# Sparse attention and a Fourier mixing layer on one core: a new issue order for the first batch's attention, Fourier stage and weight conversion

## The chip, the cores and the metric

One Trainium2 chip, one core. The time is the device time of one execution of the program in microseconds (us), and the figure for a kernel is the median of its runs.

## What is computed

Four batches of 768 tokens. Attention first (8 heads of 64): each query sees the keys less than 16 tokens away, and one summary per block of 32 tokens (the maximum of the block's keys, the mean of its values). Then a Fourier mixing layer and a two-layer network over the 512 features:

```python
scores_all = concat([where(|i-j| < 16, q@k.T/8, -1e9), q@k_sum.T/8 + log(32)])
x  = softmax(scores_all) @ concat([v, v_sum])         # per head; heads side by side: (4, 768, 512)
u  = x + real(fft(fft(x, axis=1), axis=2))
un = (u - mean(u)) / sqrt(var(u) + 1e-6)
out = u + maximum(un @ w_ch1, 0) @ w_ch2              # w_ch1 512 x 2048, w_ch2 2048 x 512, float64 in memory
```

The two weight matrices arrive as float64, and the kernel makes float32 of them by integer operations.

## The kernel before

**Attention** (`gen_attention`, L757). A batch is done in four pairs of heads, g = 0 to 3, each in three steps. First come the scores: `sc` on TensorE, their exponential on ScalarE (`p`), and a multiplication by a 0/1 mask on VectorE. Then the block sums of the values (`sum_values`, L668, or `sum_scores`), after which the next pair is prepared: `prepare` (L619) transposes k and q on TensorE (`qk`, L631 in batch 0, L639 later), ScalarE copies them out, VectorE takes the block maxima `km` (L642). Last comes the value product `av` (L676, `wide_values` in batch 0), which VectorE divides by its row sums into `x`. Batch 0 uses a wide form of the scores with the mask `wide`, later batches a narrow form with the mask `near` and a tile `vs` whose last column is set at the start (L1128, L1129). In batch 0 each pair also issues two matmuls whose result nobody reads (`keep_busy`, L750).

**Block sums of v** (`block_sums`, L560). Four heads at a time: two loads `vb` and six additions on GpSimd (POOL) into `vbs`. The load of the sums (b, gg) is issued with the values of the pair before.

**Fourier stage** (`gen_fourier`, L889). VectorE folds x into even and odd parts, once for each parity `par` (`fold`, L899 to L912). TensorE multiplies by the sequence tables `fs` (`y`, L923, L927), ScalarE copies that out (`big`), TensorE multiplies by the feature table `fd` (`mx`, L944, L946), VectorE adds to x and takes the statistics (`bst`, `norm`). The result is normalized and transposed (`unt`, L982) into `u`.

**Network** (`gen_channel`, L989). Both products are done with Winograd's form of Strassen's scheme (seven products in place of eight). It has two halves, c = 0 and 1: first four blocks j of the hidden layer (`hx`, `hy`, `hz`, L1005), then their product with w2 added to x (`ox`, `oy`, `oz`, L1052). I call them "h c=0", "o c=0", "h c=1" and "o c=1".

**Weights** (`gen_weights`, L852). There are 16 blocks, `w1_0` to `w1_7` and `w2_0` to `w2_7`. A block is made of two pieces: a load `raw` of 512 KB, two integer operations on VectorE (L820, L821), two on ScalarE (L822, L823), two more on VectorE (L825, L827) and a multiplication; four additions follow for the block (`_left_sums` or `_right_sums`). `plan` (L791) gives the order, and for each block a stage of batch 0 ahead of which it isn't issued. Batch 0 uses a block as it is made; a store to DRAM keeps it for later batches, which load it again. Three w1 blocks and four w2 blocks fit; `raw` and `vb` share four buffers.

**What sets the order.** The code is a set of generators that `drive` (L1105) advances in turns: so many steps of each in a round, some with a priority some hundred instructions ahead. A compiler's list scheduler then puts each engine's instructions into one queue, by priority and by when it takes an instruction's inputs to be there. Nearly all transfers are issued by SyncE (SP) in one such queue; an instruction at its head that waits holds all behind it. At the end of the program the order of the stages is:

```python
drive((first(attn, 6), 1, 0))                                  # L1126: pairs 0 and 1 of batch 0
...
get_tables(0)
drive((attn, 1, 0), (first(weights, 18), 3, 0))                # pairs 2 and 3 beside the conversion
...
    drive((gen_fourier(0), 4, 600), (first(weights, 16), 3, 0), (first(attn, 5), 1, 0))   # batch 1's attention
    drive((gen_channel(0), 4, 0), (weights, 12, 0), (attn, 1, 0))
```

Of the kernel before, what the change touches and what calls it, by code (L numbers as in the profile page):

```python
# [478 lines left out]
def _main_program(ctx, tc, q, k, v, moe_w_ch1, moe_w_ch2, out):  # L479
# [54 lines left out]

    def abank(shape, name):
        return psum.tile(shape, FP, tag="attn", bufs=4, name=name)
# [11 lines left out]
    nat = {}  # L548

    def load(b, g):  # L550

        qn, kn = (apool.tile([P, 2, NST // 2, 2 * D], FP, tag="nat", bufs=4, name=f"{n}n_{b}_{g}") for n in "qk")
        for dst, src in ((kn, k), (qn, q)):
            nc.sync.dma_start(out=dst.rearrange("p e j n -> p (e j) n"),
                              in_=src[b, 2 * g:2 * g + 2].rearrange("e (j p s) d -> p (e j) (s d)", p=P, s=2))
        nat[b, g] = qn, kn
# [3 lines left out]
    def block_sums(b, gg):  # L560
# [3 lines left out]
        for i in range(2):  # L564
            nc.sync.dma_start(out=raw[i].rearrange("p f d -> p (f d)"),
                              in_=v[b, 4 * gg:4 * gg + 4].rearrange("h (n f) d -> (h n) (f d)", f=BLOCK)
                              [:, hf * D * i:hf * D * (i + 1)])
        gtt(raw[0], raw[0], raw[1], ADD)
        while hf > 2:
            hf //= 2  # L570
            gtt(raw[0][:, 0:hf], raw[0][:, 0:hf], raw[0][:, hf:2 * hf], ADD)
        vb = spool.tile([4 * nb, D], FP, tag="vbs", bufs=2, name=f"vbs_{b}_{gg}")
        gtt(vb, raw[0][:, 0], raw[0][:, 1], ADD)
# [14 lines left out]
    def load_wide_values(b, g):  # L588

        vw = wide_vw(g)  # L590
        for e in range(2):
            off = v[b, 2 * g + e].offset
            parts = [(W, WK, 0, NQ), (0, W, 1, NQ)] if (b, g, e) == (0, 0, 0) else [(0, WK, 0, NQ)]
            for r0, r1, i0, i1 in parts:
                nc.sync.dma_start(out=vw[r0:r1, e, i0:i1, 0:D],
                                  in_=bass.AP(v.tensor, off + (QB * i0 - W + r0) * D,
                                              [[D, r1 - r0], [QB * D, i1 - i0], [1, D]]))

    def load_narrow_values(b, g):
# [5 lines left out]
        for e in range(2):  # L605
            off = v[b, 2 * g + e].offset
            for h in range(2):
                r, i = 64 * (e ^ h), NB2 * h
                last = (b, g, e, h) == (B - 1, NP - 1, 1, 1)
                if last:  # L610

                    nc.sync.dma_start(out=vw[r + 64 - W:r + 64, i:nb - 1, 0:D],
# [3 lines left out]
                nc.sync.dma_start(out=vw[r:r + n, i:i + NB2, 0:D],  # L616
# [59 lines left out]
    def wide_values(b, g, p, x):  # L676
        vw = wide_vw(g)
        av = [abank([P, NST, D1], f"av_{b}_{g}_{e}") for e in range(2)]
        for n in range(NQ):
            for e in range(2):  # L680
                nc.tensor.matmul(av[e][QB * (n % 2):QB * (n % 2 + 1), n // 2, :], p[:, e, n, :], vw[:, e, n, :],
                                 start=True, stop=True)
        for e in range(2):
            rc = rec[:, b * NP + g, e]
            nc.vector.reciprocal(out=rc, in_=av[e][:, :, D])
# [64 lines left out]
    def keep_busy(b, g):  # L750


        ps = bank([P, 512], f"busy_{b}_{g}")
        for _ in range(2):
            nc.tensor.matmul(ps, ident, nat[b, g][:, 0:512], start=True, stop=True)

    def gen_attention(b):  # L757
        x = bpool.tile([P, NST, DM], FP, tag="x", bufs=2, name=f"x_{b}")
        x_of[b] = x
        for g in range(NP):  # L760
# [7 lines left out]
            if b == 0:  # L768
                keep_busy(b, g)
            if n1:  # L770
                prepare(*n1)
# [6 lines left out]
            if is_wide(b):  # L778
                wide_values(b, g, p, x)
            else:  # L780
                values(b, g, *p, x)
            if n2:
                load_values(*n2)
            yield
# [6 lines left out]
    plan = [(1, 0, None), (1, 1, None), (1, 2, None), (2, 0, None), (2, 1, ("y", 0)), (2, 2, ("y", 0)),  # L791
            (2, 3, ("mx", 0)), (1, 3, ("h", 0, 0)), (1, 4, ("h", 0, 1)), (1, 5, ("h", 0, 2)), (1, 6, ("h", 0, 3)),
# [4 lines left out]
    def load_raw(upto):  # L797
        for f, j, hh in pieces[len(raws):upto]:
# [8 lines left out]
            nc.sync.dma_start(out=raw.rearrange("p (a n) w -> p a (n w)", a=a), in_=src)  # L807
# [25 lines left out]
    def make(f, j):  # L833
# [13 lines left out]
        if len(stores) > 2 or len(pieces) == len(raws):  # L847
            nc.sync.dma_start(out=stores[0][0], in_=stores.pop(0)[1])
# [3 lines left out]
    def gen_weights():  # L852
        for f, j, stage in plan:
            while stage and stage not in issued:
                yield
            yield from make(f, j)
        for to, wv in stores:
            nc.sync.dma_start(out=to, in_=wv)

    def get_w1(b, j):  # L860
# [3 lines left out]
        nc.sync.dma_start(out=w, in_=dw1[j])  # L864
        wt[1, b, j] = w

    def get_w2(b, j):
# [3 lines left out]
        nc.sync.dma_start(out=w, in_=dw2[j])  # L871
# [5 lines left out]
    def get_tables(b):  # L877
        tag, bufs = ("w1", 3) if b else ("w2", NC)
        fs = []
        for par in range(2):  # L880
            t = bpool.tile([P, 2, HT, F2 + 1], FP, tag=tag, bufs=bufs, name=f"fs_{b}_{par}")
            nc.sync.dma_start(out=t, in_=dr["fs"].ap()[par])
            fs.append(t)
        fd = bpool.tile([P, 6, HD], FP, tag=tag, bufs=bufs, name=f"fd_{b}")
        nc.sync.dma_start(out=fd, in_=dr["fd"].ap())
        tables[b] = fs, fd
        return fs, fd

    def gen_fourier(b):  # L889
# [9 lines left out]
        for par in range(2):  # L899
            sd, zw, fg = fold[:, 0], fold[:, 1], fold[:, 2 - 2 * par]  # L900
            tt(sd, x[:, 0:HT, :], x[:, HT:NST, :], SUB if par else ADD)
            tt(zw[:, :, 0:HD], sd[:, :, 0:HD], sd[:, :, HD:DM], ADD)
            tt(zw[:, :, HD:DM], sd[:, :, 0:HD], sd[:, :, HD:DM], SUB)
            nc.vector.tensor_copy(out=zq[:, par], in_=zw[:, :, Q])
# [6 lines left out]
            nc.vector.tensor_copy(out=fg[:, :, DM - 1:DM], in_=zw[:, :, HD + Q:HD + Q + 1])  # L911
            fgs.append(fg)  # L912
            yield
        big = bpool.tile([P, NC, 2, S], FP, tag="h", name=f"big_{b}").rearrange("p j h s -> p (j h s)")
# [21 lines left out]
        for half in range(2):  # L936
# [28 lines left out]
            nc.vector.scalar_tensor_tensor(out=z, in0=stat[:, :, 0], scalar=-1.0, in1=y, op0=ALU.mult, op1=ALU.mult)  # L965
# [23 lines left out]
    def gen_channel(b):  # L989
        x, u = x_of[b], wt["u", b]  # L990
        for c in range(NJ // NC):
# [44 lines left out]
            for i in range(HT):  # L1036
# [35 lines left out]
                if NC * (c + 1) == NJ:  # L1072
                    for t in (i, HT + i):
                        nc.sync.dma_start(out=out[b, P * t:P * (t + 1), :], in_=x[:, t, :])
# [10 lines left out]
    load(0, 0)  # L1085
    nc.scalar.dma_start(out=count, in_=dr["count"].ap())
    nc.scalar.dma_start(out=wide, in_=dr["wide"].ap())
# [39 lines left out]
    nc.sync.dma_start(out=near, in_=dr["near"].ap().rearrange("p (h i) c -> p h i c", h=2))  # L1127
    nc.vector.memset(vs, 0.0)  # L1128
    nc.vector.tensor_scalar(out=vs[:, :, D], in0=half_of, scalar1=float(BLOCK), scalar2=None, op0=ALU.mult)  # L1129
    get_tables(0)  # L1130
    drive((attn, 1, 0), (first(weights, 18), 3, 0))
    for b in range(B):
        attn = gen_attention(b + 1) if b + 1 < B else iter(())
        if b == 0:
            drive((gen_fourier(0), 4, 600), (first(weights, 16), 3, 0), (first(attn, 5), 1, 0))
# [56 lines left out]
```

## Time and profile before

| | |
|---|---|
| median of 5 runs | 881.01 us |
| lowest, highest | 876.55, 888.2 us |
| the profiled execution | 888.29 us |
| its span, first to last instruction | 886.5 us |
| mean granted TensorE clock | 0.971 |
| TensorE busy | 829.2 us (94%) |
| VectorE busy | 499.5 us (56%) |
| ScalarE busy | 229.6 us (26%) |
| GpSimd busy | 47.9 us (5%) |
| first `y` matmul of batches 0, 1, 3 | 76.44, 305.91, 704.46 us |

Times in the profile count from the span's first instruction. A row of the timeline gives the start, the length, the engine, the line, the operation with the tile written and the tiles read, how many instructions are merged, and in brackets how long the engine had been idle and what ended that. In a table by stretches, (x12) is the number of instructions that began there, PEclk is the granted TensorE clock (1.00 is full), and the DMA share is that of the core's 16 DMA engines. One matmul on float32 counts as two or more instructions.

### The profile page before, as it was taken

The page shows a single profiled execution, that of the slowest core. Times are in us where ns is not written, and L with a number is a line of the kernel's source. Part 1 is how long each engine was busy: PE and PEld are TensorE (multiplying, and loading weights), DVE is VectorE, ACT ScalarE, POOL GpSimd, SP SyncE. Part 2 cuts the span into 40 slices and gives each one's busy share as a digit, 9 for nine tenths or more (in the row PEclk, how much of TensorE's full clock was granted, in tenths as well). Part 3 has the DMA queues.
Part 4 walks back from the last instruction along what each step waited for, and adds up shares of the span by engine and source line. Part 5 has one row for each costly group of instructions (what it writes and reads, how often), then busy time and mean ns, then how long its engine had stood idle before and what let it go on. Part 6 is the DMA issues. An engine that isn't in the chain of part 4 may idle for free. (4 is left out here: it accounts for less than half of the span.)

```text
span 886.5 us, 14658 instructions
## 1 busy us (share of the span) xinstructions
PE 829.2 (94%) x6122; PEld 612.7 (69%) x6122; DVE 499.5 (56%) x1107; ACT 229.6 (26%) x473; POOL 47.9 (5%) x48
## 2 busy tenths in 40 slices
PE   5976898899969998999999998999999989999997
PEld 3755665578538886678758886678758876687586
DVE  2479979796898347354329347353329355442352
ACT  2563354641530034312020034310120022101200
POOL 2400103002040000000000000000000000000000
PEclk8988979999998999999999999999999999999999
DMA  9997757893762284251531293220421261304001
GB/s 215 199 297 163 186 200 182 274 300 133 220 208 95 81 288 115 96 143 37 160 137 60 73 295 79 84 84 1 173 90 60 91 248 42 125 1 188 20 26 50
DMA packets 99915, 122.33 MB, mean 138 GB/s; under 512 B 50208, under 2 KB 83200, under 8 KB 99840
## 3 DMA queue, kind: packets, MB, share of 16 engines
q1 hardware_dynamic: 99152, 120.75, 46.1%
q8 instruction: 50, 0.82, 0.4%
q10 hardware_dynamic: 688, 0.56, 0.2%
q14 instruction: 25, 0.20, 0.1%
HBM read 100.32 MB, written 20.97 MB: 137 GB/s over the span
## 5 line engine op out<-in xcount | busy, mean ns | idle before, releaser
L1005 PE MATMUL hx<-u,w 128*128 128x384 f32 x512 | 186.5, 495 | 9.5 <-DVE h L542 4.2
L1005 PEld LDWEIGHTS hx<-u,w 128*128 128x128 f32 x512 | 95.7, 192 | 78.1 <-DVE h L542 7.8
L1005 PE MATMUL hz<-u,w 128*128 128x384 f32 x256 | 95.8, 493 | 3.3 <-ACT h L1022 2.3
L1052 PE MATMUL oz<-w,s 128*128 128x256 f32 x384 | 91.5, 379 | 0.0
L1052 PE MATMUL ox<-w,s 128*128 128x256 f32 x384 | 91.4, 381 | 0.0
L1052 PE MATMUL ox<-w,h 128*128 128x256 f32 x384 | 90.5, 384 | 0.0
L1052 PEld LDWEIGHTS ox<-w,h 128*128 128x128 f32 x384 | 74.0, 193 | 12.2 <-issue 0.6
L542 DVE TENSOR_TENSOR x<-ox,x 128x256 f32<-128x256 f32 x96 | 40.5, 423 | 71.8 <-PE ox L1052 71.6
L1052 PEld LDWEIGHTS ox<-w,s 128*128 128x128 f32 x384 | 72.2, 190 | 11.3 <-DVE x L542 1.4
L1052 PEld LDWEIGHTS oz<-w,s 128*128 128x128 f32 x384 | 72.9, 190 | 10.0
L1005 PEld LDWEIGHTS hz<-u,w 128*128 128x128 f32 x256 | 48.8, 192 | 37.9 <-ACT h L1022 3.0
L542 DVE TENSOR_TENSOR h<-hy,h 128x384 f32<-128x384 f32 x32 | 17.8, 555 | 60.6 <-PE hy L1005 60.6
L1005 PE MATMUL hy<-u,w 128*128 128x384 f32 x128 | 46.5, 486 | 0.0
L929 ACT COPY big<-y 128x192 f32<-128x192 f32 x32 | 10.7, 335 | 137.5 <-PE y L923 137.5
L542 DVE TENSOR_TENSOR h<-hx,h 128x384 f32<-128x384 f32 x32 | 17.8, 556 | 50.4 <-PE hx L1005 49.4
L1052 PE MATMUL oy<-w,h 128*128 128x256 f32 x192 | 45.6, 380 | 0.0
L923 PE MATMUL y<-fs,fold 128*128 128x193 f32 x192 | 36.7, 341 | 6.3 <-DVE fold L908 6.3
L1015 ACT COPY h<-hx 128x384 f32<-128x384 f32 x32 | 15.3, 479 | 98.3 <-PE hx L1005 94.0
L1052 PEld LDWEIGHTS oy<-w,h 128*128 128x128 f32 x192 | 36.5, 191 | 5.1
L923 PEld LDWEIGHTS y<-fs,fold 128*128 128x128 f32 x192 | 32.3, 195 | 9.4 <-DVE fold L908 6.5
L542 DVE TENSOR_TENSOR x<-oz,x 128x256 f32<-128x256 f32 x48 | 20.4, 424 | 32.8 <-PE oz L1052 32.7
L1031 ACT ACTIVATE h<-hx 128x384 f32<-128x384 f32 x32 | 15.7, 491 | 87.1 <-PE hx L1005 87.1
(115 smaller groups left out, 1106.7 us busy)
## 6 DMA issues: line engine op xcount, KB each, us to landing
w<-dw SPq DMA_DIRECT2D x48, 896.0 KB, 5.5
raw<-in_moe_w_ch_dram SPq DMA_DIRECT2D x32, 512.0 KB, 5.5
dw<-w SPq DMA_DIRECT2D x16, 896.0 KB, 7.0
vw<-in_v_dram SPq DMA_DIRECT2D x47, 192.0 KB, 4.9
kn<-in_k_dram SPq DMA_DIRECT2D x16, 384.0 KB, 5.7
qn<-in_q_dram SPq DMA_DIRECT2D x16, 384.0 KB, 6.4
vb<-in_v_dram SPq DMA_DIRECT2D x16, 384.0 KB, 5.2
out_dram<-x SPq DMA_DIRECT2D x24, 256.0 KB, 2.0
```

The source lines that it names most:

```text
L542: nc.vector.tensor_tensor(out=out, in0=in0, in1=in1, op=op)
L923: nc.tensor.matmul(y, fgs[par][:, st, P * g:P * (g + 1)], fs[par][:, g % 2, st, :], start=(st == 0), stop=(st == HT - 1))
L929: nc.scalar.copy(out=ty[:, g, par:S2:2], in_=y[:, 0:F2])
L1005: nc.tensor.matmul(ps, w[:, a, kk, :], u[:, r, kk, :], start=start and kk == 0, stop=stop and kk == 1, skip_group_check=True)
L1015: nc.scalar.copy(out=c11, in_=X)
L1031: nc.scalar.activation(out=c21, in_=X, func=AF.Relu)
L1052: nc.tensor.matmul(ps, left[a][:, n, :], wt[2, b, j][:, r, :], start=start and n == 0, stop=stop and n == NC - 1, skip_group_check=True)
```

## The change

- Batch 0's four `keep_busy` calls go. A new `keep_busy` issues two such matmuls after each of two folding steps of the first parity of batch 0's Fourier stage.
- For the last pair of batch 0, the value product is issued ahead of `prepare` of batch 1's first pair, and `tc.issue_after` puts that pair's TensorE instructions behind the last `av` matmul in TensorE's queue. It sets the order only; it adds no wait.
- Pairs 2 and 3 of batch 0 get a priority 600 ahead of the conversion. The second weight block is issued only behind the last folding instruction, and `w1_2`, `w2_0`, `w2_1`, `w2_2`, `w2_3` only behind the last instruction of the normalization (VectorE's queue; order only). `w1_3` moves ahead of `w2_1`.
- The block sums for batch 1 move from GpSimd to VectorE, as one addition and one `tensor_reduce`. Those of other batches stay.
- The setting of `vs` (L1128, L1129) is put behind pair 1's value product in VectorE's queue.
- Every transfer on SP up to the end of the first Fourier stage keeps the program's order (`tc.keep_in_program_order`). The first two raw loads move ahead to pair 0, the next two ahead of the tables; `near` goes behind the tables; `wide` moves from ScalarE's queue to SP's.

```diff
+    in_order = [True]
+    def fetch(out, in_):
+        ins = nc.sync.dma_start(out=out, in_=in_)
+        if in_order[0]:
+            tc.keep_in_program_order(ins)
...
         vb = spool.tile([4 * nb, D], FP, tag="vbs", bufs=2, name=f"vbs_{b}_{gg}")
-        gtt(vb, raw[0][:, 0], raw[0][:, 1], ADD)
+        if b == 1:
+            tt(raw[0], raw[0], raw[1], ADD)
+            nc.vector.tensor_reduce(out=vb, in_=raw[0].rearrange("p f d -> p d f"), op=ADD, axis=AX.X)
+        else:
+            gtt(raw[0], raw[0], raw[1], ADD)
...
+        marks["last av"] = ins.ins
...
-    def keep_busy(b, g):
-        ps = bank([P, 512], f"busy_{b}_{g}")
-        for _ in range(2):
-            nc.tensor.matmul(ps, ident, nat[b, g][:, 0:512], start=True, stop=True)
...
-            if b == 0:
-                keep_busy(b, g)
+            early = (b, g) == (0, NP - 1)
+            if early:
+                wide_values(b, g, p, x)
             if n1:
-                prepare(*n1)
+                with tc.issue_after(marks["last av"]) if early else ExitStack():
+                    prepare(*n1)
...
             if n2:
                 load_values(*n2)
+            if (b, g) == (0, 0):
+                load_raw(2)
...
-    plan = [(1, 0, None), (1, 1, None), (1, 2, None), (2, 0, None), (2, 1, ("y", 0)), (2, 2, ("y", 0)),
-            (2, 3, ("mx", 0)), (1, 3, ("h", 0, 0)), (1, 4, ("h", 0, 1)), ...
+    plan = [(1, 0, None), (1, 1, ("fold", 0)), (1, 2, ("mx", 0)), (2, 0, ("mx", 0)), (1, 3, ("h", 0, 0)), (2, 1, ("mx", 0)),
+            (2, 2, ("mx", 0)), (2, 3, ("mx", 0)), (1, 4, ("h", 0, 1)), ...
...
-            yield from make(f, j)
+            steps = make(f, j)
+            while True:
+                with tc.issue_after(marks[stage]) if stage in marks else ExitStack():
+                    done = next(steps, steps) is steps
...
+    def keep_busy(b, par, t):
+        if (b, par) == (0, 0):
+            ps = bank([P, DM], "busy")
+            for i in range(2):
+                nc.tensor.matmul(ps, ident, t[:, i, :], start=True, stop=True)
...
             tt(sd, x[:, 0:HT, :], x[:, HT:NST, :], SUB if par else ADD)
+            keep_busy(b, par, sd)
             tt(zw[:, :, 0:HD], sd[:, :, 0:HD], sd[:, :, HD:DM], ADD)
             tt(zw[:, :, HD:DM], sd[:, :, 0:HD], sd[:, :, HD:DM], SUB)
+            keep_busy(b, par, zw)
...
+        marks["fold", b] = ins.ins
+        issued.add(("fold", b))
...
     load(0, 0)
+    fetch(out=wide, in_=dr["wide"].ap())
     nc.scalar.dma_start(out=count, in_=dr["count"].ap())
-    nc.scalar.dma_start(out=wide, in_=dr["wide"].ap())
...
     drive((first(attn, 6), 1, 0))
-    nc.sync.dma_start(out=near, in_=dr["near"].ap().rearrange("p (h i) c -> p h i c", h=2))
-    nc.vector.memset(vs, 0.0)
-    nc.vector.tensor_scalar(out=vs[:, :, D], in0=half_of, scalar1=float(BLOCK), scalar2=None, op0=ALU.mult)
+    with tc.issue_after(marks["av", 0, 1]):
+        nc.vector.memset(vs, 0.0)
+        nc.vector.tensor_scalar(out=vs[:, :, D], in0=half_of, scalar1=float(BLOCK), scalar2=None, op0=ALU.mult)
+    load_raw(4)
     get_tables(0)
-    drive((attn, 1, 0), (first(weights, 18), 3, 0))
+    fetch(out=near, in_=dr["near"].ap().rearrange("p (h i) c -> p h i c", h=2))
+    drive((attn, 1, 600), (first(weights, 18), 3, 0))
...
-            drive((gen_fourier(0), 4, 600), (first(weights, 16), 3, 0), (first(attn, 5), 1, 0))
+            drive((gen_fourier(0), 4, 600), (first(weights, 66), 12, 0), (first(attn, 5), 1, 0))
+            in_order[0] = False
             drive((gen_channel(0), 4, 0), (weights, 12, 0), (attn, 1, 0))
```

All other `nc.sync.dma_start` calls of this program become `fetch` with the same arguments. `marks` also records the first reciprocal after each value product and the last instruction of the normalization.

## The prediction, made before the changed kernel was run

> **What bounds the kernel now.** First the page: engine totals, then the slices.
>
> ```profile
> PE 829.2 (94%) x6122; PEld 612.7 (69%) x6122; DVE 499.5 (56%) x1107; ACT 229.6 (26%) x473; POOL 47.9 (5%) x48
> ...
> DVE  2479979796898347354329347353329355442352
> PEclk8988979999998999999999999999999999999999
> ```
>
> A slice is 22.2 us. TensorE bounds the whole, but in slices 3 to 12 (about 45 to 265 us) VectorE is full, and the granted clock is lowest there. The first `y` matmuls of batches 1 and 2 are 198.6 us apart (305.91, 504.46); from batch 0's (76.44) to batch 1's it is 229.5 us. So the loss sits in the first 306 us. The table by stretches says where:
>
> ```profile
> 20.00:40.00 20.00, 20.00 (x298) 14.55 (x300) 7.49 (x16) 9.08 (x17) 7.65 (x7) 0.95 0.94 188
> 40.00:53.00 13.00, 13.00 (x194) 9.20 (x191) 7.06 (x12) 6.49 (x13) 3.31 (x5) 1.00 1.06 335
> 53.00:70.00 17.00, 10.57 (x171) 7.68 (x169) 15.72 (x36) 11.81 (x20) 0.14 (x1) 0.80 1.22 255
> 70.00:90.00 20.00, 13.72 (x68) 10.93 (x66) 19.47 (x35) 7.73 (x21) 3.04 (x2) 0.83 0.73 145
> 90.00:122.00 32.00, 28.11 (x304) 23.51 (x304) 26.30 (x78) 12.18 (x25) 2.88 (x4) 0.79 0.64 175
> 122.00:160.00 38.00, 34.30 (x294) 19.49 (x296) 33.44 (x63) 19.86 (x41) 8.68 (x5) 0.96 0.77 225
> 160.00:187.00 27.00, 23.66 (x293) 14.65 (x285) 24.82 (x55) 19.29 (x37) 0.00 (x0) 1.00 0.91 253
> 187.00:220.00 33.00, 33.00 (x158) 28.79 (x161) 25.47 (x56) 6.41 (x11) 5.13 (x5) 1.00 0.65 212
> 220.00:268.00 48.00, 40.81 (x221) 23.30 (x221) 42.30 (x79) 22.23 (x43) 10.79 (x8) 0.96 0.69 214
> ```
>
> The columns after the length are PE, PEld, DVE, ACT, POOL busy. Until 53 us TensorE has no gap and VectorE is idle over half the time (batch 0's attention). From 53 to 90 us TensorE is idle 12.7 of 37 us while VectorE is full: conversion competes with the end of attention and the fold. From 122 to 187 us both are nearly full; TensorE idles 7.0 us. In 187 to 220 us TensorE is full ("o c=0") and VectorE idles 7.5 us. The timeline shows what starts late:
>
> ```profile
> 12.21 1.99 DVE L1129 TENSOR_SCALAR vs<-half 128x2 f32<-128x2 f32 x1 [10.88 <-DMA half<-c_half]
> 15.11 1.35 PE L662 MATMUL sc<-qt,km 64*32 64x384 f32 x4 [3.96 <-DVE km L642]
> 31.68 1.98 PE L755 MATMUL busy<-qt,ident 128*128 128x512 f32 x4
> 48.15 1.24 PE L658 MATMUL sc<-qt,kt 64*96 64x64 f32 x24
> 57.65 0.85 PE L639 MATMUL qk<-ident,kn 128*128 128x128 f32 x6 [3.31 <-ACT cvt L822]
> 59.87 1.51 PE L639 MATMUL qk<-ident,qn 128*128 128x128 f32 x6 [1.37 <-DMA qn<-in_q_dram]
> 62.50 2.87 PE L681 MATMUL av<-vw,p 128*64 128x65 f32 x46 [0.57 <-ACT kt L641]
> 69.67 1.75 DVE L542 TENSOR_TENSOR fold<-x 128x1536 f32<-128x1536 f32 x1
> 76.44 2.94 PE L923 MATMUL y<-fs,fold 128*128 128x193 f32 x8 [6.28 <-DVE fold L908]
> 86.88 2.35 POOL L545 TENSOR_TENSOR vb<-vb,vb 96x1024 f32<-96x1024 f32 x1 [21.32 <-DMA vb<-in_v_dram]
> 86.91 2.61 DVE L821 TENSOR_SCALAR cvt<-raw 128x512 int32<-128x512 int32 x1
> ```
>
> A load that isn't needed (`half`) holds VectorE's queue, so the first `km` is 4 us late. The last `av` stands behind batch 1's `qk`, whose k and q are still in flight (`qn`, issued at 50.13, lands at 59.87; `kn`, issued 2.1 us ahead of it, fits 57.6, so I don't believe the ACT step named). The fold waits for that `av`, then `y` for the fold. And while POOL adds, a VectorE step of 0.42 us takes 2.61.
>
> **What the Trainium skill says.** "SBUF — State Buffer", section "Who interferes with whom": VectorE and GpSimd share a port pair under an exclusive lock, and `tensor_reduce` on trn2 never contends. The trace agrees on the lock (0.42 against 2.61 us); it has no `tensor_reduce` beside POOL work. "TensorE: Matmul & The Clock Gate", Part 1: after an idle window of about 3.4 us the clock is halved until a busy one. The trace agrees: after 6.28 us idle, 8 `y` matmuls take 2.94 us, against 1.58 in batch 3. "DMA: Bandwidth & Descriptors", section "Issuing engines are not separate DMA queues": transfers from ScalarE's and SP's queues share the same 16 engines, so moving `wide` should save issue time only. The before trace can't test that.
>
> **The change, part by part.**
>
> *Start and pair 0.* Without L1129 ahead, `km` is ready at 9.1 us instead of 15.1, and the first pair's scores end 4 us earlier. `keep_busy` of pair 0 is 3.06 us more. But the block sums now come last: POOL ends them at 17.25, so `vs` moves from 22.92 only to about 17.3. Gain 5.6. *Pairs 1 and 2*: a period is 10.33 us with TensorE gapless, ScalarE at 4.9 and VectorE at 4.3 us; taking out 1.98 us leaves TensorE the bound: 2 x 1.98 = 4.0. Scores of pair 3 start at 48.15 - 9.6 = 38.6.
>
> *Pair 3.* Its `vw` copy ends 6.3 us after its scores start; `av` 1.6 and the division 1.3 follow: x is complete 9.2 us after, against 69.4 - 48.15 = 21.3 now. Gain 12.1; sum 21.7. The cover to check is DMA. Up to pair 3's values SP must bring k, q 3.1 MB, v 2.4, block loads 2.4, `wide` and `sel` 0.5, and now the first raw pieces 1.0 ahead of them: 9.4 MB, landing at 40 us with the mean 235 GB/s, at 50 with the 188 of the slow stretch; needed at 45. I allow 2 us: x complete at 49.7, lead 19.7.
>
> *Fold and `y`.* The first parity's fold takes about 5 us without foreign work (6.8 less 2.3 that was mixed in): `y` starts at 55. The two new `keep_busy` calls (4 us) lie in TensorE's gap. The second parity follows at 62.5, `y` ends at about 68, against 88.9. Then `mx` to the end of normalization takes 17 us in batch 3 (715 to 731.6), undisturbed, against 27.4 here (88.5 to 116). I take 18.5 for `w1_1` and the block sums beside it: 86.5, and with 6 us of transposes the network starts at 93 instead of 121.7. Lead 28.7.
>
> *What is owed.* A block costs VectorE 2 x (0.42 + 0.42 + 0.69 + 0.68 + 0.68) + 4 x 0.42 = 7.5 us. Eight pieces, four blocks, are converted before 121.7 now. With the new plan it is `w1_0` (in attention's idle VectorE time), `w1_1`, and some 0.4 of `w1_2`: 2.4 blocks. The 1.6 missing ones cost 12 us where VectorE is full. Lead 16.7 when the eighth block is ready (now 163).
>
> *After that.* With `w1_3` ahead of `w2_1` to `w2_3`, the last block of "h c=0" no longer waits for all eight, and `w1_4` to `w1_6` slide under "o c=0", where VectorE idles 7.5 us. I take 5.5 (0 to 7.5). From "o c=0" on (220 to 268) nothing changes: the w2 buffers come free only then. Lead 22.2.
>
> *Edits at about nothing.* Batch 1's sums on VectorE: 1.2 us (1024 at the 1.75/1536 of the fold row) plus 1.25 (from 0.95 for the 768 of the `km` row), twice. The first pair lies in idle time; the second replaces 3.8 us that POOL's lock now adds at 86.9 to 92. Without that cover: 2.5. `near` is needed first at about 60. New waits: on SP the third raw load waits for a buffer and behind it stand tables, `near`, and batch 1's k, q and v; `y` and `qk` would wait. On VectorE the second sum may wait for its load with the fold behind it. Both between 0 and 10 us; I take 0 beyond the 2 allowed.
>
> Sum against the profiled execution: 888.3 - 22 = 866. It lies 7.3 us over the median; the parts are differences of one trace, so from 881 I get 859.
>
> **The rivals.**
> *More passes through.* If VectorE, full from 50 us, loses fewer gaps than the 13% it idles between 60 and 268 us now, the debt shrinks: at 5% idle it saves another 10 (8% of the 125 us from 93 to about 218): 849. For it: uncontended stages fill better. Against: `norm`'s short steps and buffer waits stay. The ceiling is TensorE, 55 + 198.6, far off.
> *The front is held by loads.* `kn` of batch 1 stands behind tables and raw pieces, and `y` behind its `qk`: x is in time, but `y` starts at about 65, and half the lead is lost: 870. For it: `qn` took 9.7 us here.
> *The clock.* Without `keep_busy` gaps halve the clock in pairs 1 to 3: each has 6.4 us of matmuls without queueing, doubled that is 3 x 6.4 = 19 us more: 859 + 19 = 878. Against: TensorE stays gapless by the sums above.
> *Slower: SP's fixed order serializes the pieces.* In the fixed stretch six pieces (`w1_1`, `w1_2`, `w2_0`) are loaded; if each load sits behind a waiting transfer of batch 1 until the conversion before it is done, each exposes its 5.5 us landing: 6 x 5.5 = 33, 892. Four exposed pieces cancel the gain, six make it slower. Against: four buffers let two to three pieces run ahead.
>
> **How the numbers follow.** The sum 45%, more through 25%, loads 15%, clock 7%, serialized 8%. About 1% (8.8 us) is what a measurement of this kernel can tell from no change. Faster: 45 + 25 + 12 of the loads' 15 = 82%; same: the clock's 7 and the loads' other 3, 10%; slower 8%. The range leaves out the serialized case, the clock and part of the edges: low 845 (more through, plus 4), high 873 (loads, plus 3).
>
> **What would show it.** Right: last `av` of batch 0 ahead of `qk` at about 45 us; fold at 50, `y` at 55 with no conversion between; first `hx` at about 93; first `ox` near 150; batch 1's `y` near 284. Wrong: a VectorE or SP wait on `vb` or `raw` over 5 us between 45 and 90, or a clock under 0.9 before 45.

## The result, and the profile after

The changed kernel takes 880.15 us (median of 42 runs, 876.5 to 885.53), the kernel before 882.0 us (median of 79 runs beside it, 871.61 to 888.69). The ratio is 1.000, with a 95% interval of 0.9988 to 1.0013 (the two medians alone give 0.998): no change, or 2 us at most, where I forecast 859. The changed kernel's profiled execution has a span of 878.8 us. Ratios everywhere, and the median of *early only*, leave out slow runs, those more than 1.5% above the fastest of their kernel.

The profiled execution of the kernel before that the prediction used (span 886.5) lies 6 us over its kernel's median. I ran that kernel again unchanged ("before again": 882.81 us, span 881.0) and compare with this second trace wherever it matters. Its first `y` of batch 1 comes at 300.6 us, where the first trace has 305.9 and the changed kernel 300.1: what looked like a gain of 5.8 us in the first batch is a difference between two executions of one kernel.

The page of the changed kernel: engine totals, then the slices of 22 us.

```profile
PE 823.1 (94%) x6114; PEld 608.2 (69%) x6114; DVE 505.4 (58%) x1111; ACT 229.5 (26%) x473; POOL 36.7 (4%) x38
...
DVE  3588996899999257353239247354329355442252
PEclk9979999799999999999999999999999999999999
```

TensorE's busy time and share hardly move. VectorE is still nearly full from slice 3 to slice 13, to about 290 us. The table by stretches, with the same columns as in the prediction:

```profile
40.00:53.00 13.00, 12.68 (x154) 9.35 (x156) 8.66 (x20) 7.54 (x13) 0.14 (x1) 0.87 0.58 129
53.00:70.00 17.00, 11.44 (x79) 7.66 (x80) 16.97 (x33) 2.33 (x7) 0.14 (x1) 0.80 1.07 281
70.00:90.00 20.00, 19.22 (x163) 15.48 (x165) 16.04 (x32) 7.92 (x22) 0.00 (x0) 1.00 0.90 173
90.00:122.00 32.00, 29.57 (x442) 20.33 (x436) 29.72 (x81) 22.67 (x44) 0.00 (x0) 0.95 0.77 213
122.00:160.00 38.00, 33.24 (x303) 19.58 (x302) 30.01 (x58) 20.87 (x41) 6.02 (x5) 0.96 0.68 188
160.00:187.00 27.00, 21.75 (x177) 15.12 (x177) 23.50 (x54) 12.94 (x24) 0.00 (x0) 0.81 0.99 276
220.00:268.00 48.00, 44.68 (x155) 28.55 (x153) 45.74 (x89) 22.39 (x43) 5.38 (x4) 1.00 0.76 254
```

From 70 to 122 us TensorE now idles 3.2 us where it idled 10.2, at a higher clock. From 160 to 187 it is worse: 21.75 us busy where it was 23.66, at clock 0.81 where it was 1.00. The timeline of the same execution:

```profile
18.20 0.52 PE L685 MATMUL vs<-vbs,sel 96*32 96x64 f32 x4 [4.75 <-POOL vbs L553]
...
53.26 1.90 DVE L580 TENSOR_REDUCE vbs<-vb 96x64 f32<-96x1024 f32 x1
...
57.95 1.75 DVE L550 TENSOR_TENSOR fold<-x 128x1536 f32<-128x1536 f32 x1
...
59.75 4.31 PE L914 MATMUL busy<-fold,ident 128*128 128x512 f32 x6 [5.56 <-DVE fold L550]
...
63.69 0.16 DVE L940 COPY fold<-fold 128x3 f32<-128x3 f32 x1
...
63.90 1.15 PE L954 MATMUL y<-fs,fold 128*128 128x193 f32 x6
...
130.74 2.53 POOL L553 TENSOR_TENSOR vb<-vb,vb 96x1024 f32<-96x1024 f32 x1 [76.33 <-DVE cvt L839]
...
130.98 2.85 DVE L550 TENSOR_TENSOR w<-cvt 128x512 f32<-128x512 f32 x1
...
137.92 2.93 PE L1038 MATMUL hx<-u,w 128*128 128x384 f32 x4 [3.08 <-ACT h L1048]
...
148.99 0.95 DVE L655 TENSOR_REDUCE km<-kt 128x24 f32<-128x768 f32 x1 [4.06 <-ACT kt L654]
...
171.24 0.90 PE L652 MATMUL qk<-ident,kn 128*128 128x128 f32 x3 [1.78 <-ACT kt L654]
...
171.94 2.77 PE L1038 MATMUL hx<-u,w 128*128 128x384 f32 x4
...
277.58 3.62 PE L1085 MATMUL ox<-w,s 128*128 128x256 f32 x8 [3.71 <-DVE x L550]
```

The fold starts at 57.95 (before 69.67) and `y` at 63.9 (before 76.44), so the front is earlier. Later come the losses: a VectorE step (L550, `w`) of 2.85 us beside GpSimd's sum, and TensorE waiting 3.08 us soon after it; VectorE standing 4.06 us behind `km`; TensorE waiting on ScalarE's `kt` and then running at half clock (four `hx` instructions in 2.77 us, where 1.56 us is usual; the four at 137.92 the same); and 3.71 us of waiting in "o c=1".

Milestones of the three traces, in us (first or last matmul of the stage, from the timeline):

| | before, shown | before again | after | lead on "again" |
|---|---|---|---|---|
| first `y` | 76.4 | 76.0 | 63.9 | 12.1 |
| last `y` ends | 88.9 | 88.3 | 80.0 | 8.3 |
| first `hx` | 121.7 | 121.0 | 106.2 | 14.8 |
| first `ox` (o c=0) | 175.5 | 174.8 | 158.4 | 16.4 |
| "o c=0" ends | 220.0 | 219.3 | 216.0 | 3.3 |
| "h c=1" ends | 268.2 | 262.4 | 255.6 | 6.8 |
| batch 1's first `y` | 305.9 | 300.6 | 300.1 | 0.5 |

The lead is there until the first `ox`. Inside "o c=0" 13.1 us of it go. About 2 of these are moved work: the value products of batch 1's last pair, which the kernel before runs just behind that stage, lie inside it in the changed kernel. "h c=1" gives 3.5 back, and "o c=1" takes 6.3.

A ledger shows what kind of loss this is. In each stretch of 4 us I take TensorE's loss as the stretch's length less the product of busy time and granted clock, and sum it up to 300 us:

| trace | loss to 120 us | loss 120 to 300 us | sum | span |
|---|---|---|---|---|
| before, shown | 39.6 | 19.1 | 58.7 | 886.5 |
| before again | 40.0 | 13.7 | 53.7 | 881.0 |
| after | 25.1 | 25.3 | 50.3 | 878.8 |

Against before again the front takes 14.9 us of loss out, and 11.6 us come back. The stretches in which they come back are 160 to 180 us (8.2 against 2.5), 120 to 140 (4.2 against 1.4) and 260 to 280 (6.9 against 2.7); the others sum to 1.2 us the other way. The first trace has 6.5 us in the last of these, so there the ledger alone proves nothing. The milestones do: from the end of "h c=1" to the first `y` the changed kernel takes 44.5 us, and both traces of the kernel before about 38.

### The profile page after: what moved, and what is told of

The parts are those of the page before. It is cut to its first block, busy times and chain, and to the rows that moved or that the text cites. A ratio compares the mean times of both kernels' runs of the same rounds, so it can differ in the third digit from the quotient of the medians.

```text
span 878.8 us, 14637 instructions
## 1 busy us (share of the span) xinstructions
PE 823.1 (94%) x6114; PEld 608.2 (69%) x6114; DVE 505.4 (58%) x1111; ACT 229.5 (26%) x473; POOL 36.7 (4%) x38
## 5 line engine op out<-in xcount | busy, mean ns | idle before, releaser
L1085 PE MATMUL ox<-w,s 128*128 128x256 f32 x384 | 93.5, 387 | 5.2 <-DVE x L550 5.2
L550 DVE TENSOR_TENSOR x<-ox,x 128x256 f32<-128x256 f32 x96 | 40.3, 421 | 69.3 <-PE ox L1085 69.1
L550 DVE TENSOR_TENSOR h<-hy,h 128x384 f32<-128x384 f32 x32 | 17.8, 556 | 61.0 <-PE hy L1038 60.9
L550 DVE TENSOR_TENSOR h<-hx,h 128x384 f32<-128x384 f32 x32 | 17.8, 556 | 48.2 <-PE hx L1038 48.2
L655 DVE TENSOR_REDUCE km<-kt 128x24 f32<-128x768 f32 x16 | 15.2, 951 | 45.7 <-ACT kt L654 32.8
L1064 ACT ACTIVATE h<-hx 128x384 f32<-128x384 f32 x32 | 15.7, 490 | 85.8 <-PE hx L1038 85.8
L550 DVE TENSOR_TENSOR x<-oz,x 128x256 f32<-128x256 f32 x48 | 20.3, 423 | 30.9 <-PE oz L1085 30.9
```

The lines of the kernel that those rows point to most:

```text
L550: nc.vector.tensor_tensor(out=out, in0=in0, in1=in1, op=op)
L655: nc.vector.tensor_reduce(out=km[:, 0:nb], in_=kt[:, W:W + S].rearrange("p (n f) -> p n f", f=BLOCK), op=ALU.max, axis=AX.X)
L1064: nc.scalar.activation(out=c21, in_=X, func=AF.Relu)
L1085: nc.tensor.matmul(ps, left[a][:, n, :], wt[2, b, j][:, r, :], start=start and n == 0, stop=stop and n == NC - 1, skip_group_check=True)
```

## The experiments

**First theory: the withheld conversion is a debt on VectorE.** At the first `hx` the kernel before has converted eight pieces, the changed one four, and the sixteenth piece is ready at 166.3 (165.6 in before again) and 166.2 us. (I count a piece as ready at the end of its last step before the multiplication.) A lead of 15 us would be paid with two blocks of 7.5 us. *light before* and *light after* leave the conversion out of both kernels:

```diff
-        nc.vector.tensor_scalar(out=ex, in0=high, scalar1=0x7FF00000, scalar2=None, op0=ALU.bitwise_and)
...
-        tt(dst, tmp[:, 1, :], tmp[:, 0, :], ALU.mult)
+        nc.vector.tensor_scalar(out=dst, in0=raws[i].bitcast(FP)[:, :, 1], scalar1=0.01, scalar2=None, op0=ALU.mult)
```

Of *before again* (the kernel before, unchanged):

> The kernel before, unchanged, for a second profile, because its profiled execution lay 7 us over its median and batch 1's first y matmul at 305.91 us there against 300.09 in the changed kernel. Theory (the change gains nothing because the conversion owed is paid back on VectorE): batch 1's y at about 300 to 302 us, and the sixteenth converted piece at about 165 us as in the first profile. Rival (the change gained 5.8 us in the first batch and lost it later): y at 305 to 306 again.

Of *light before*:

> The kernel before with the conversion left out: in place of its seven steps per piece, VectorE multiplies the high half of each number, read as a float32, by 0.01 (one step of about 0.4 us), so the weights are not the reference's; loads, sums and stores stay. It takes 32 x 2.5 = 79 us off VectorE. Theory: the first batch is bound by VectorE's conversion, so this is 15 to 35 us faster than before (about 850 to 866). Rival (the first batch is bound by TensorE and its order): under 8 us faster.

Of *light after*:

> The changed kernel with the conversion left out in the same way. Theory (the lead of 15.5 us at the first hx is lost only because two blocks more are still to be converted): with nothing owed the lead stays, and this is 10 to 16 us faster than the kernel before with the conversion left out. Rival (the lead is lost to TensorE's own work, which is merely done in another order): within 4 us of it.

Measured: light before 862.65 us, ratio to before 0.977 [0.9727, 0.9813]; light after 862.78, ratio 0.9767 [0.9717, 0.9817]. Conversion beside the rest costs about 20 us in one kernel and 17 in the other. My expectation for light after missed, but the run does not test the debt by its total: its front lost 33.0 us up to 120 where the changed kernel lost 25.1, so that it had no lead at its first `hx` (112.9 against 109.8).

*owed light* tests the debt itself. Only the four pieces that the changed kernel has not converted at its first `hx` (`w1_2`, `w2_0`) are made light:

```diff
+        if 4 <= i < 8:
...
+            nc.vector.tensor_scalar(out=dst, in0=raw.bitcast(FP)[:, :, 1], scalar1=0.01, scalar2=None, op0=ALU.mult)
...
+            return
```

> The changed kernel, with one multiplication in place of the seven steps for the four pieces of w1_2 and w2_0 (those weights are then not the reference's). These four pieces are the ones that the kernel before has done ahead of its first hx and the changed kernel has not. Theory (the lead at the first hx is eaten by these pieces on VectorE): first hx stays within 3 us of 106, the time from the first hx to batch 1's first y falls from 193.9 us to 178-182, total 863-869 us. Rival (the stretch is longer for other reasons: the order of batch 1's attention, the clock): at least 188 us for that stretch, total 875-880.

Measured: 879.54 us, ratio 0.998 [0.9963, 0.9997]; 192.1 us from the first `hx` to batch 1's first `y` (193.9 in the changed kernel). The theory fell: both figures are the rival's. A piece needs 0.42 + 0.42 + 0.69 + 0.68 + 0.68 = 2.89 us of VectorE, a light one 0.42, so four pieces free 9.9 us; yet the sixteenth piece comes at 164.2, only 2.0 us earlier. VectorE's waits from 104 to 168 us tell why:

```profile
DVE h L550 <- PE hx L1044: 7.4, 2, 3.9
DVE km L655 <- ACT kt L654: 4.1, 1, 4.1
```

In the changed kernel the same two rows are 1.9 and 4.1 us; all of VectorE's waits in this time sum to 15.7 us here and 9.0 there. VectorE's queue is fixed, and `h` additions and a `km` stand in it ahead of the next pieces; without the four pieces VectorE waits there for TensorE and ScalarE. Most of the freed time turns into waiting.

**The front alone.** *early only* is the kernel before with a single edit of the change, the last value product ahead of batch 1's keys.

```diff
+            early = (b, g) == (0, NP - 1)
+            if early:
+                wide_values(b, g, p, x)
...
```

> The kernel before with one part of the change: the last value product of batch 0 ahead of batch 1's keys. Theory: x is complete 3-6 us earlier and so is the first y, but VectorE has the same conversion left; the lead at the first hx is under 4 us and batch 1's first y moves by under 2 us: total 879-885 us. Rival (an earlier x is worth its full amount): 875-878.

Measured: 886.5 us, ratio 1.005 [1.0021, 1.0079], slower, which neither case of the expectation had. The first `y` is at 63.6, as early as with the whole change, but the first piece of weights is converted at 70.2 (before 56.5) and the sixteenth at 177.1 (before 166.3), and the first `ox` comes at 185.2 (before 175.5). Here an earlier fold pushed the conversion back, and the network waited for it.

*ungated* keeps the change but no longer withholds conversion:

```diff
-    plan = [(1, 0, None), (1, 1, ("fold", 0)), (1, 2, ("mx", 0)), (2, 0, ("mx", 0)), (1, 3, ("h", 0, 0)), (2, 1, ("mx", 0)),
-            (2, 2, ("mx", 0)), (2, 3, ("mx", 0)), ...
+    plan = [(1, 0, None), (1, 1, None), (1, 2, None), (2, 0, None), (1, 3, ("h", 0, 0)), (2, 1, ("y", 0)),
+            (2, 2, ("y", 0)), (2, 3, ("mx", 0)), ...
```

> The changed kernel with the stages of the plan as before (w1_1, w1_2, w2_0 without a stage, w2_1 and w2_2 behind y), so conversion is no longer withheld from the fold and the normalization; the order of blocks and all else stay. Theory (a piece costs VectorE 3.75 us wherever it is put): first hx moves later by about 3.7 us for each piece done ahead of it, 110-120 us, batch 1's first y and the total stay: 877-884 us. Rival 1 (withholding leaves VectorE idle 4 us in 70-90): 873-877. Rival 2 (the withheld conversion is what gives the front its worth): 886 or more.

Measured: 887.54 us (879.77 to 891.82), ratio 1.005 [1.0027, 1.0072]; its profiled execution (881.07) is among its lowest and can't show where the typical one loses. Rival 2 of the expectation holds: withholding conversion is worth some 7 us to this front by the medians, and 4 by the ratios.

**Which stall eats the lead in "o c=0"?** *w2 light* makes the six pieces of `w2_1` to `w2_3` light (`10 <= i < 16` in the edit of owed light).

> The changed kernel with one multiplication in place of the seven steps for the six pieces of w2_1, w2_2 and w2_3 (those weights are then not the reference's). Theory (o c=0 starts at 158 us with only part of its w2 blocks there, and TensorE meanwhile runs batch 1's last pair alone): the three blocks are there by 155, TensorE's loss to gaps and clock at 160-200 falls from 9.7 us to under 4, total 868-874. Rival (as with the owed pieces, less conversion only leaves VectorE waiting in its queue): loss at 160-200 of 8 or more, total 877-881.

Measured: 872.07 us, ratio 0.9887 [0.9863, 0.9911]. The stretch of "o c=0" in it:

```profile
160.00:187.00 27.00, 25.98 (x215) 21.21 (x215) 25.82 (x58) 10.10 (x19) 0.00 (x0) 1.00 0.94 271
```

TensorE is busy 25.98 us at full clock, where the changed kernel has 21.75 at 0.81. Six pieces free 14.8 us of VectorE and the total falls by 8; four pieces of the blocks before them freed 9.9 and gave about 1. So "o c=0" starts at 158 us with two of its four w2 blocks there, and TensorE then runs batch 1's last pair of heads, one short product after another, each waiting on ScalarE or VectorE. That the late blocks are what it waits for is argued from their times; the run also gives VectorE the 14.8 us for other work. (The last light piece is written at 159.4, not by 155 as expected.)

*w1_3 last* puts `w1_3` behind `w2_3` again:

```diff
-    plan = [..., (1, 3, ("h", 0, 0)), (2, 1, ("mx", 0)), (2, 2, ("mx", 0)), (2, 3, ("mx", 0)), ...
+    plan = [..., (2, 1, ("mx", 0)), (2, 2, ("mx", 0)), (2, 3, ("mx", 0)), (1, 3, ("h", 0, 0)), ...
```

> The changed kernel with w1_3 behind w2_3 again, as in the kernel before. My step 'After that' gave this move the larger part of 5.5 us. If so: 882-886. Theory (the eighth block comes at the same time whichever is last, and the loss is only shifted from h c=0 to o c=0): h c=0 ends 8-14 us later, o c=0 is 8-14 us shorter, total 876-882. Rival (with all w2 blocks there o c=0 runs without gaps and the lead survives): 868-874.

Measured: 880.28 us, ratio 0.9969 [0.9952, 0.9986]. The first `ox` moves from 158.4 to 173.5, so "h c=0" ends later than the expected 8 to 14 us, and "o c=0" is 8.6 us shorter (49.0 against 57.6). TensorE now waits once, 8.25 us at 146.55 in "h c=0". The total says that the order of these blocks only decides in which stage the eighth one is waited for.

*km after 12* moves one instruction: `km`, behind which VectorE stood 4.06 us, goes behind the twelfth piece.

```diff
-        nc.vector.tensor_reduce(...
+        with tc.issue_after(marks["piece", 11]) if (b, g) == (1, 3) and ("piece", 11) in marks else ExitStack(): nc.vector.tensor_reduce(
...
```

> The changed kernel with one instruction moved: in VectorE's queue the block maxima km of batch 1's last pair, which wait for kt until 149 us, go behind the twelfth piece's conversion instead of ahead of it (TensorE's order is the same instruction for instruction). Theory (VectorE's queue stands still behind km, and w2_1 to w2_3 with it): piece 12 done by 141-146 us instead of 153, piece 16 by 157-162 instead of 166, batch 1's first y 2-5 us earlier, total 875-879. Rival (the loss of 8 us at 160-180 lies in TensorE's own order, where batch 1's attention stands alone): batch 1's first y within 1.5 us of 300, total 879-882.

Measured: 880.31 us, ratio 0.9973 [0.9961, 0.9984]. The twelfth piece ends at 151.7 instead of 153.1, because the wait only changed its name: VectorE's next step of that piece waits 5.68 us for ScalarE (L834), which copies `kt` and `qt` first. The figures are the rival's, but the run removes one of two stalls in series, so it decides nothing between the theories.

*wprio* gives the conversion a priority of 300 in batch 0's network stage, and so puts it ahead of attention on all engines:

```diff
-            drive((gen_channel(0), 4, 0), (weights, 12, 0), (attn, 1, 0))
+            drive((gen_channel(0), 4, 0), (weights, 12, 300), (attn, 1, 0))
```

> The changed kernel with conversion 300 ahead in priority in the network stage of batch 0, so that the rest of batch 1's attention comes behind it on all engines (its last km behind the twenty-second piece). Theory (attention put ahead of conversion and alone on TensorE eats the lead): eighth block by 150-160 us, TensorE's loss to gaps and clock at 160-180 falls from 8 to under 4 us, total 868-876. Rival (the same losses come back where the attention then stands, in o c=1 and batch 1's Fourier stage): 877-885.

Measured: 890.42 us, ratio 1.0088 [1.0063, 1.0113], slower than either case of the expectation. The sixteenth piece is ready at 157.8, 8.4 us earlier, as the theory wanted, but TensorE's own order has not followed:

```profile
176.78 1.46 PE L727 MATMUL ss<-qt,km 64*32 64x384 f32 x2 [15.76 <-DVE km L655]
```

TensorE waits 15.76 us for the `km` that now stands behind eleven more pieces. With batch 3's sums on VectorE as well (below) this kernel takes 887.7, ratio 1.0048 [1.0032, 1.0064], slower than all three cases of its expectation:

> wprio_300 with batch 3's block sums on VectorE too. If both theories hold the gains add: 862-870 us. If priority of the conversion is worth nothing, the gain of the sums alone stays: 873-877. If the later attention takes the place where the sums gained, 875-881.

**The block sums, and GpSimd's lock.** The change moves only batch 1's sums to VectorE. *vsum 13* also moves batch 3's, *vsum all* those of batches 1 to 3, *psum 1* moves batch 1's back, *vsum 3* moves batch 1's back and batch 3's over; *before v3* and *before vall* do the same in the kernel before for batch 3, and for batches 1 to 3.

```diff
-        if b == 1:
+        if b in (1, 3):
```

This is vsum 13; the others made from the changed kernel have `b >= 1`, `b == 3` or no batch in this place. The two made from the kernel before put the changed kernel's VectorE form beside GpSimd's.

> The changed kernel with batch 3's block sums on VectorE too (b in (1, 3)). In the changed kernel's trace GpSimd's additions for batch 3 at 262 to 275 us stretch VectorE's steps, and TensorE waits 2.46 and 3.71 us for them, then runs at half clock for about 3.5 us. If that lock is what the wait is: 5 to 8 us faster than the changed kernel, so 873 to 876 and faster than before too. If VectorE's 3.1 us for each sum only move the wait: within 2 us of 880.

> The kernel before with batch 3's block sums on VectorE (one addition and one reduction) and nothing else. Theory (GpSimd's lock in o c=1, where VectorE is full, costs 6 us in both kernels): 874-878 us, batch 1's first y 4-8 us earlier. Rival (the gain of 1% came only with the changed front): 880-884.

> The changed kernel with batch 1's block sums back on GpSimd. My step put this edit at about nothing. If so: 878-883 us. Theory of the lock (what GpSimd adds beside a full VectorE costs some 3 us a pair of sums): first hx 2-6 us later than 106, total 882-888. Rival (the sums on VectorE lie in the path of the fold and the normalization, so taking them off helps): 872-877.

> The changed kernel with batch 1's block sums back on GpSimd and batch 3's on VectorE. The two single edits gained 4 us (batch 1 back) and 7 us (batch 3 over): if they add, 868-872. If the gain of the first was only another order, 873-877.

> The changed kernel with the block sums of batches 1, 2 and 3 on VectorE. In it batch 2's sums on GpSimd stretch VectorE's steps at 131-137 us, ahead of a TensorE wait of 3.1 us. If the lock is dearer than the 6.2 us of VectorE that two pairs of sums cost, 870-873 us; if not, 874-878 (batch 3's gain alone gave 874.2).

> The kernel before with the block sums of batches 1, 2 and 3 on VectorE and nothing else of the change. The changed kernel with the same edit measured 865.6. Theory (GpSimd's lock is what ate the lead of the changed front; without it part of the lead stays): 870-876 here. Rival (the front is worth nothing with or without the lock, and the whole gain of 2% is the sums): 863-868.

| sums on VectorE | in the kernel before | in the changed kernel |
|---|---|---|
| none | 882.0, ratio 1 | psum 1: 877.83, 0.9953 [0.9937, 0.997] |
| batch 1 | not run | 880.15, 1.000 [0.9988, 1.0013] |
| batch 3 | before v3: 876.5, 0.9929 [0.9912, 0.9947] | vsum 3: 875.74, 0.9924 [0.99, 0.9948] |
| 1 and 3 | not run | vsum 13: 874.21, 0.9904 [0.987, 0.9937] |
| 1, 2 and 3 | before vall: 872.65, 0.9899 [0.9851, 0.9946] | vsum all: 865.59, 0.9802 [0.9772, 0.9831] |

A row with two figures has both kernels with the same sums on VectorE, so it shows what the rest of the change is worth: 0.5% with none moved, nothing with batch 3's, and some 1% with all three. The change as I made it gains nothing because moving batch 1's sums takes back what the rest gains (psum 1 against the change; the intervals don't meet).

vsum 13, before v3 and before vall came as the theory had them. psum 1 lies between the range for no effect and that for a gain, and against the theory of the lock. vsum 3 came as its second case: the two gains don't add. vsum all went 4 us under its best case: it beats both kernels by 2%. Its table by stretches:

```profile
122.00:160.00 38.00, 35.48 (x376) 21.65 (x374) 33.34 (x71) 23.00 (x45) 0.00 (x0) 1.00 0.80 224
160.00:187.00 27.00, 22.17 (x138) 16.91 (x135) 24.86 (x57) 11.73 (x22) 0.00 (x0) 0.94 0.96 263
250.00:300.00 50.00, 49.51 (x329) 41.92 (x327) 28.19 (x59) 8.81 (x24) 0.00 (x0) 1.00 0.48 157
```

and the kernel before with the same edit:

```profile
122.00:160.00 38.00, 37.21 (x314) 20.99 (x314) 37.20 (x77) 24.32 (x49) 0.00 (x0) 1.00 0.81 243
160.00:187.00 27.00, 25.96 (x291) 19.16 (x290) 25.55 (x59) 13.47 (x25) 0.00 (x0) 1.00 1.00 273
250.00:300.00 50.00, 50.00 (x338) 41.90 (x337) 29.27 (x61) 7.13 (x20) 0.00 (x0) 1.00 0.41 149
```

The GpSimd column (the last of the busy times) is at 0, and from 250 to 300 us TensorE is full in both (49.51 and 50.00 of 50; the changed kernel had 43.83). In vsum all the first `ox` is at 154.1 and batch 1's first `y` at 284.1. Its stretch from 160 to 187 is still weak (22.17 at clock 0.94 against 25.96 at 1.00): the late w2 blocks, untouched. The ledger for these traces, with the second column split:

| trace | to 120 us | 120-160 | 160-200 | 200-260 | 260-300 | sum | span |
|---|---|---|---|---|---|---|---|
| before again | 40.0 | 5.2 | 3.4 | 2.5 | 2.7 | 53.7 | 881.0 |
| after | 25.1 | 6.0 | 9.7 | 2.1 | 7.5 | 50.3 | 878.8 |
| w2 light | 24.3 | 3.5 | 1.0 | 7.2 | 7.6 | 43.5 | 870.1 |
| vsum all | 26.0 | 2.5 | 6.5 | 0.4 | 0.5 | 35.8 | 864.5 |
| before vall | 34.3 | 0.8 | 1.0 | 1.0 | 0.0 | 37.1 | 867.8 |

Against before again the sums of the last three fall by 10.2, 17.9 and 16.6 us and the spans by 10.9, 16.5 and 13.2, so the ledger accounts for the larger part in each. It also parts the two causes. From 160 to 200 us light w2 blocks take out 8.7 us of the change's loss and the moved sums 3.2. From 260 to 300 the moved sums take out 7.0 and light w2 blocks nothing. (Light w2 blocks have a new loss of 7 us at 200 to 220.) And in vsum all 7.1 of the 8.3 us that its front gains on before vall still come back, 5.5 of them from 160 to 200: most of this lead is lost without GpSimd's sums too.

How moving the sums gains is shown only in part. GpSimd's additions stretch single VectorE steps (next section). But VectorE's busy time over the whole kernel hardly moves, 505.4 us in the change and 502.3 in vsum all, 498.9 in before again and 499.1 in before vall: the sums cost VectorE about what the stretched steps did. What differs is where it falls. In vsum all batch 3's additions on VectorE (1.2 us each) stand at 270 us, and its reductions (1.9 us each) only at 320 and 405 us, behind the 300 us in which the losses lie. No run separates this from the other order that each edit gives VectorE's queue, or from the shared `raw` and `vb` buffers coming free at other times.

The six runs of before vall lie in two groups, 869.53 to 870.14 and 875.15 to 876.66, and its profiled execution is in the lower. So by medians the rest of the change is worth 7 us once all three batches are moved, by the traces 3.

The single edits don't add. Batch 1's sums back on GpSimd gain 0.5% on the change, which I can't explain, and nothing once batch 3's are on VectorE (vsum 3 against vsum 13). Each of these kernels has a schedule of its own, so I read nothing into differences of 2 or 3 us between their profiled executions.

*vsum 13 last* asks whether the place of the wait for the eighth block matters without GpSimd's sums in "o c=1" (vsum 13 with `w1_3` behind `w2_3`):

> Batch 3's sums on VectorE, with w1_3 behind w2_3. Theory (where the eighth block is waited for makes no difference): 872-877 us, as with batch 3's sums alone. Rival (only one of the two places is hidden once GpSimd's lock is gone): 866-871 or 879 and more.

Measured: 873.57 us, ratio 0.9899 [0.987, 0.9928], the same as vsum 13. It doesn't.

## Why the prediction was wrong, step by step

Two things failed. The front's terms were mis-sized: the lead at the first `hx` was 15.5 us and not 28.7. And at the step *What is owed* all of it went: I had the eighth block of weights 16.7 us earlier, and it came when it did before. Step by step:

*Start and pair 0.* I had 5.6 us; pair 1's scores start at 24.38 where they started at 27.48, a gain of 3.1. The block sums did come last, as forecast, but without `keep_busy` TensorE stood 4.75 us behind them (the row at 18.20) and ran at clock 0.84 from 15 to 20 us and 0.82 from 20 to 25. I had put that gap at nothing beyond its length.

*Pairs 1 and 2, pair 3.* The mechanism was right: the last `av` ends at 54.2, ahead of batch 1's `qk`, and the fold starts 11.7 us earlier. I had 19.7. Pairs 1 to 3 took 29.8 us (24.38 to 54.2) where my periods sum to 24.6, part of it at clock 0.87 (the row 40 to 53). So of the rival "clock" a part came true, and with it the sign "a clock under 0.9 before 45". VectorE's queue put a vbs reduction (1.90 us, at 53.26) and conversion steps ahead of the last division. The cover that I named for the sums, "the first pair lies in idle time", was not there, and the reduction costs 1.90 us, not 1.25.

*Fold and y.* From fold to `y` 6.0 us (5.3 forecast). The new `keep_busy` filled TensorE from 59.75 to 63.9, but held nothing up: the fold's last step for this `y` ends on VectorE at 63.85. The `y` stage took 16.1 us, not 13, and from there to the first `hx` 26.2, not 25. So the lead at the first `hx` was 15.5 on the shown trace, not 28.7: 8.0 us lost up to the fold, 0.7, 3.1 and 1.2 in these three.

*What is owed.* The lead at the eighth block was to be 16.7 us and was 0: 15.5 us were paid, not 12. So the amount was nearly right and its mechanism wrong. I counted the missing pieces' VectorE time as a debt where "VectorE is full". owed light took 9.9 us of that work away, and the sixteenth piece came 2.0 us earlier and the total fell by about 1. What counts is which block is waited for: the four pieces ahead of "h c=0" were nearly free, the six ahead of "o c=0" were worth 8 us.

*After that.* Forecast 5.5 us more for `w1_3` ahead of `w2_1`; w1_3 last measured nothing for it. The move let "o c=0" start with two of its four w2 blocks, and 13.1 us of lead went inside that stage. 'From "o c=0" on (220 to 268) nothing changes' failed too: "h c=1" gave 3.5 us back and "o c=1" took 6.3, against before again.

*Edits at about nothing.* Batch 1's sums, which I put at nothing, cost the change about 0.5% (psum 1). I costed the sums that move and left those that stay out of the account. Batch 2's first sum now falls at 130.7 to 137.1 us, amid "h c=0": VectorE steps of 0.68 and 0.42 us take 2.85 and 1.48 there, and TensorE waits 3.08. In the Trainium skill, "SBUF — State Buffer", section "Who interferes with whom", has a VectorE step with two inputs from SBUF contend with GpSimd, and one with a single input only in a two-port mode. The step of 2.85 us has two inputs and agrees; the one of 1.48 has one, and the trace doesn't show its mode. Moving the sums of batches 2 and 3 gains the changed kernel 2%, moving those of batches 1 to 3 gains the kernel before 1%. With all of them moved the changed kernel has batch 1's first `y` at 284.1, where the prediction has 284. That agreement is luck: the terms of the lead were off, and the sums that gave it were not among them.

*The rivals.* No load held the front: the fold waited for VectorE's own queue and `y` for the fold. VectorE waited nowhere on `vb` or `raw` for over 5 us between 45 and 90. Yet the sign that I named for this rival came true on SP, which stood 5.5 us at a `raw` load until VectorE's first sum freed the buffer, and 11.2 us behind `qk` in one wait; so the sign was a bad one. The serialized pieces did not come: the ninth to sixteenth piece keep the pace of before. "More through" did not come either.

*Readings.* Three statements ahead of the result were wrong besides, and none carries the sum. The first `y` of batch 2 is at 505.70 in the first trace, not 504.46. A block sum is five additions, not six. And that trace does have a `tensor_reduce` beside GpSimd's work:

```profile
14.12 0.94 DVE L642 TENSOR_REDUCE km<-kt 128x24 f32<-128x768 f32 x1
14.26 2.59 POOL L545 TENSOR_TENSOR vb<-vb 96x512 f32<-96x512 f32 x3
```

It takes 0.94 us there and 0.95 alone, so it is not stretched.

What stays open: how much of the stall in "o c=0" is the late w2 blocks and how much is VectorE's time that light blocks free for other work; how much of the gain from moving the sums is GpSimd's lock; and why batch 1's sums are better left on GpSimd. Why the sixteenth piece comes at the same time before and after is only argued: queue orders tie VectorE to TensorE's pace in "h c=0". That it agrees to 0.1 us is chance, since before again has it 0.7 us earlier.

## What to carry to other kernels

A lead at an early stage is worth what the next stages can take: before you credit it, ask of each later stage which input comes last, and test it by making that input free. A queue that is fixed before the run turns freed work into waiting, so a debt counted in instruction times can be wrong by its whole amount. Count what an edit leaves in place, too: GpSimd's sums beside a full VectorE fell under critical stages, and moving them was worth 2% to the changed kernel, where the whole front was worth 1% at best.

## What the runs showed of the hardware that I had not expected

- A reduction on VectorE over the strided inner axis (96x1024 into 96x64, f32) takes 1.90 us, 1.86 ns for each element; the block maxima over a contiguous axis (128x768) take 0.95 us, 1.24 ns for each.
- The block sums of four heads take GpSimd 6.3 us beside a busy VectorE (130.74 to 137.08) and VectorE 3.1 (1.21 + 1.90).
- After 5.56 us without work, six instructions of the new `keep_busy` took 4.31 us; four of the old ones took 1.98. The first three started 1.02, 0.85 and 0.85 us apart, the next two 0.57 and 0.43, and the `y` instructions behind them 0.16 us apart, as in batch 3 of the first trace (0.17). So work meant to raise the clock is itself slow when it begins after the gap, and here it was over before `y`. The Trainium skill's "TensorE: Matmul & The Clock Gate", Part 1, has the clock halved after an idle window of about 3.4 us; this gap agrees.
